# One written order for attention and all gate products, maxima kept in PSUM, and the pooled v of five pairs on VectorE

## The chip, the cores and the metric

The kernel runs on one core of a Trainium2 chip. A time is the device time of one execution in microseconds (us). Named engines: PE (TensorE, matmuls; PEld its weight loads), DVE (VectorE), ACT (ScalarE), POOL (GpSimd) and SP (SyncE, which here only issues DMAs).

## The reference, cut to what matters

```python
# attention: B=2, H=8, S=576, D=64; factor 4
out = repeat(softmax_attn(mean4(q), mean4(k), mean4(v)), 4)      # pooled over 4 positions
out += local_attn(q, k, v, mask=|i-j| < 4)                       # narrow band
x = out reshaped to [1152, 512]
# gate stage, d_ff 1536 (the weights are float64)
x = (silu(x @ w_gate) * (x @ w_val)) @ w_out
# 8 experts, all of them for every token: d_ff 1024
P = softmax-like routing of x @ w_gate2, normalised 8 times over rows and columns
out = sum_e P[:, e] * (relu(x @ w1[e]) @ w2[e])
```

## The kernel before, in words

**Attention.** The 16 heads are worked as 8 pairs, each pair on 128 partitions. For a pair, PE makes two banks of local scores (`s0`, `s1`: five windows of 64 each) and one bank of pooled scores (`s2`). `most` (L494) takes their maxima on DVE and scales them into the exponent's bias `stb`; `exps` (ACT) makes the exponentials and their sums; `sums` (DVE) makes the reciprocals `rs`; `share` (POOL, L527) scales the exponentials; `turn` (PE) transposes them, `turned` (ACT) copies them out; `values` (PE) multiplies with v; `wide` (ACT) and `joined` (DVE, L583) put both attentions together; `upper` (ACT) and `lower` (DVE, L600) split the result into two float16 halves `xhl`, the operand of the gate products. Pooled k is made by DVE, pooled q by DVE for pairs 0 and 2 and by POOL for the others, pooled v (`pool_v`, L472, three additions) by POOL for all pairs.

**Gate products.** There are 12 blocks of 128 gate and 128 value columns. A block's weights arrive as float64 bit patterns and are converted in steps: `a` (ACT), `b`, `c`, `d` (DVE, L240/L238, L241, L244, L247), `e` (ACT, maximum), `p`, `q`, `m` (scale), `h` (ACT, upper half), `l` (DVE, lower half, L299). The tokens are worked in two chunks: c=0 with 512 and c=1 with 640 columns. A product is 12 matmuls for c=0 and 24 for c=1, gate and value apart; ACT takes the gate out of PSUM (L658), DVE the value (L659).

**What sets the order.** `PLAN` (L59) is an order written out by hand for attention, the conversion of the first four blocks, and three early blocks of c=0 (`y0`, `y1`); `in_order` (L100) makes every engine keep it. The names in it are a step and a pair or block (`s03` is `s0` of pair 3, `pv2` the pooled v of pair 2, `ga1` step `a` of block 1). `fill` (L120) puts matmuls without use ahead of some steps, as listed in `FILL` (L58). Behind the plan a loop (L799) emits the remaining gate products with conversions, and a list scheduler orders them, with `high_priority` for the copies out of PSUM. Then `act_split` splits the gate stage's result and `w_out` multiplies it with `w_out`; the experts follow.

Of the kernel before, what the change touches and what calls it, by code (L numbers as in the profile page):

```python
# [44 lines left out]
NX = 3  # L45
# [14 lines left out]
K0 Q0 K1 Q1 K2 Q2 Z0 W0 W1 Z1 W2 kd0 qd0 s00 kd1 s10 m00 s20 qd1 m10 s01 e00 kd2 K3 Q3 m20 W3 s11 m01  # L60
e10 qd2 s21 m11 e20 s02 m21 K4 pv0 Q4 e01 R0 r0 s12 m02 e11 g0 s22 m12 e02 m22 kd3 pv1 t0 e21 c0 qd3 r1
xg0 e12 kd4 g1 e22 o0 xm0 qd4 r2 xp0 t1 w0 Z2 xr0 K5 j0 pv2 Q5 s03 xu0 c1 R1 W4 s13 u0 m03 g2 ga0 l0 o1
m13 gb0 e03 s23 pv3 Z3 gc0 w1 t2 e13 K6 Q6 j1 s04 W5 c2 qd5 m23 gd0 s14 u1 e23 m04 o2 l1 ge0 m14 r3 ga1
kd5 s24 R2 g3 W6 gp0 w2 Z4 m24 e04 K7 gq0 Q7 kd6 pv4 W7 gm0 e14 t3 j2 gb1 gh0 s05 qd6 e24 gl0 s15 c3 m05
r4 s25 ga2 m15 g4 o3 gc1 e05 m25 u2 gd1 t4 pv5 e15 l2 s06 kd7 c4 qd7 s16 gb2 e25 m06 w3 gc2 ge1 s26 j3
R3 m16 Z5 u3 o4 r5 e06 m26 g5 l3 gp1 e16 xg1 Z6 gd2 pv6 gq1 w4 gm1 e26 t5 j4 gh1 xm1 s07 r6 ge2 gl1 g6
xp1 s17 c5 xr1 m07 xu1 gp2 ga3 s27 gq2 m17 o5 u4 gm2 tu0 l4 e07 m27 y01 pv7 Z7 w5 tl0 e17 j5 gb3 u5 t6
# [11 lines left out]
def tile_kernel(ctx, tc, qT, kT, vw, vd4, wgv, wo, wg2, w1, w2, out):  # L79
# [144 lines left out]
    def f64_steps(raw, nm, relu):  # L224
# [24 lines left out]
        return f, (size, place, high, low)  # L249
# [17 lines left out]
    def gv_steps(f):  # L267
# [226 lines left out]
    def most(i, pr):  # L494
        ps, mx, bs = sps[pr, i], stm[pr % 2], stb[pr % 2]
        if i < 2:
            V.tensor_reduce(mx[:, i * NW:(i + 1) * NW], ps[:, :NW * WS].rearrange("p (u w) -> p u w", u=NW),
                            axis=AX.X, op=ALU.max)
            if i:
                V.tensor_scalar(bs[:, :2 * NW], mx[:, :2 * NW], -QK, None, op0=ALU.mult)  # L500
        else:
            w = slice(2 * NW, 2 * NW + NQB)
            V.tensor_reduce(mx[:2 * HQ, w], ps[:2 * HQ, :DW].rearrange("p (u w) -> p u w", u=NQB), axis=AX.X, op=ALU.max)
            V.tensor_scalar(bs[:2 * HQ, w], mx[:2 * HQ, w], -QKD, None, op0=ALU.mult)
# [103 lines left out]
    gv_done = {}  # L608
    gv_act = {}

    def gv_step(c, f, early):
        o, nh = CH[c]
        if f == 0:
            amx[c] = cp.tile([P, KF1], F32, name=f"amx{c}")
        iv = wp.tile([P, 2], F32, tag="iv", bufs=6, name=f"iv{c}_{f}")
        with tc.high_priority():
            V.tensor_scalar(iv[:, 0:1], gv_inv[f], x1s[c][1], 0.5 if early else 1.0, op0=ALU.mult, op1=ALU.mult)
            if early:
                V.tensor_scalar(iv[:, 1:2], iv[:, 0:1], 2.0, None, op0=ALU.mult)
# [15 lines left out]
        if early:  # L635
# [7 lines left out]
            def value():  # L643
                gv_done[c, f] = V.scalar_tensor_tensor(x, pp[1], iv[:, 1:2], x, op0=ALU.mult, op1=ALU.mult)

# [3 lines left out]
                    "y1": lambda: run(1), "yd": value, "yj": finish}  # L649
        else:  # L650
            pp = []
            for t in range(2):
                ps = ps_mm(f"gv{c}_{f}_{t}")[:, :nu, :n]
                for u in range(nu):
                    products(ps[:, u], t, u)
                pp.append(ps)
# [321 lines left out]
```

## Time and profile before

| | us |
|---|---|
| median of 3 timed runs (1017.86 to 1021.94) | 1019.16 |
| the profiled execution | 1013.1 |
| its span, first to last instruction | 1011.3 |
| PE busy in the span | 993.1 (98%) |
| DVE busy | 752.3 (74%) |
| ACT busy | 439.7 (43%) |
| POOL busy | 79.5 (8%) |

Busy time is a mean over very different stages, so it is read stage by stage: attention until about 98 us, the gate products until 225, `w_out` until 299, the experts until the end. [...] POOL's spans are rough.

### The profile page before, as it was taken

What the parts mean: (1) busy time and instruction counts of PE and PEld (TensorE: products, weight loads), DVE (VectorE), ACT (ScalarE), POOL (GpSimd) and SP (SyncE); (2) the same over time, 40 slices, a digit from 0 to 9 for tenths busy, and PEclk for the clock granted to TensorE, in tenths of its full rate; (3) what the DMA queues carried; (4) which work ended last, traced back from release to release, by engine and by line L of the source; (5) the groups of instructions that cost most, each with busy time, mean ns of one, the idle gap of its engine ahead of it and who ended that gap; (6) DMA issues with size and microseconds to landing.
All of it is one profiled execution on the core that took longest, in us unless ns stands there. A gap on an engine that the chain in (4) does not pass through costs nothing.

```text
span 1011.3 us, 16420 instructions
## 1 busy us (share of the span) xinstructions
PE 993.1 (98%) x6612; PEld 621.8 (61%) x6612; DVE 752.3 (74%) x1521; ACT 439.7 (43%) x913; POOL 79.5 (8%) x97
## 2 busy tenths in 40 slices
PE   8889999999999999999999999999999999999998
PEld 6675655664667666557556655755666575565644
DVE  6999888857938998797497588849748884973721
ACT  6776775656517463452154145215314521541200
POOL 5871000000002000000000000000000000000000
PEclk9979999999999999999999999999999999999999
DMA  9831342410200221121103012110301211010011
GB/s 291 278 112 54 125 158 94 167 42 1 84 1 1 84 84 42 43 84 42 42 1 126 1 42 84 43 42 5 121 1 42 84 43 42 25 60 1 1 42 53
DMA packets 12988, 67.97 MB, mean 67 GB/s; under 512 B 1456, under 2 KB 1840, under 8 KB 6512
## 3 DMA queue, kind: packets, MB, share of 16 engines
q1 hardware_dynamic: 12912, 66.92, 18.7%
q8 instruction: 52, 0.85, 0.3%
q14 instruction: 24, 0.20, 0.1%
HBM read 64.55 MB, written 2.36 MB: 66 GB/s over the span
## 4 chain that ended last, share of the span: by engine, by line
PE 80%; DVE 12%; ACT 3%; DMA 3%; issue 1%; SPq 0%; POOL 0%; DVEq 0%; ACTq 0%; POOLq 0%
PE y L212 37%; PE p L212 32%; PE gv L212 7%; PE wo L212 3%; DVE cvg L244 1%; DVE gv L299 1%; DMA v<-in_vd 1%; DVE w L205 1%; DMA vz<-in_vw 1%; DMA rawo<-in_wo 1%; DVE xhl L604 1%; DVE cvg L241 1%; DVE ahl L205 1%; DVE cvg L247 1%; DVE act L659 0%
## 5 line engine op out<-in xcount | busy, mean ns | idle before, releaser
L212 PE MATMUL y<-w,hhl 128*128 128x512 f16 (+1 forms) x1752 | 395.7, 376 | 0.0
L212 PE MATMUL p<-bop,w 128*128 128x320 f16 (+1 forms) x2688 | 353.5, 286 | 0.6 <-ACT s L863 0.4
L212 PEld LDWEIGHTS <-w 128*128 128x128 f16 x2688 | 262.9, 98 | 90.2 <-issue 2.0
L212 PEld LDWEIGHTS <-hhl 128*128 128x128 f16 x1752 | 171.5, 98 | 178.9
L874 ACT ACTIVATE hhl<-h 128x640 f16<-128x640 f32 (+1 forms) x128 | 83.1, 676 | 158.1 <-DVE h L846 158.0
L212 PE MATMUL gv<-xhl,gv 128*128 128x320 f16 (+1 forms) x864 | 141.9, 326 | 3.6 <-DVE act L659 1.9
L204 ACT ACTIVATE w<-r,s_w 128x256 f16<-128x256 f32 (+1 forms) x96 | 71.1, 783 | 121.5 <-PE y L212 86.3
L905 DVE SCALAR_TENSOR_TENSOR acc<-y,pe,acc 128x512 f32<-128x512 f32 (+1 forms) x64 | 47.4, 740 | 101.3 <-PE y L212 100.5
L212 PEld LDWEIGHTS <-gv 128*128 128x128 f16 x864 | 84.2, 98 | 59.4 <-issue 3.1
L875 DVE SCALAR_TENSOR_TENSOR hhl<-h,hhl 128x640 f16<-128x640 f32 (+1 forms) x128 | 94.2, 753 | 18.5 <-ACT hhl L874 17.2
L846 DVE SCALAR_TENSOR_TENSOR h<-p,u 128x256 f32<-128x256 f32 (+1 forms) x192 | 85.0, 453 | 20.4 <-PE p L212 14.8
L205 DVE SCALAR_TENSOR_TENSOR w<-r,s_w,w 128x256 f16<-128x256 f32 (+1 forms) x96 | 78.3, 835 | 16.8 <-ACT w L204 16.7
L212 PE MATMUL wo<-ahl,wo 128*128 128x320 f16 (+1 forms) x416 | 70.9, 327 | 0.1
L846 DVE SCALAR_TENSOR_TENSOR u<-p,u 128x320 f32<-128x320 f32 (+1 forms) x128 | 57.6, 450 | 4.4 <-PE p L212 3.4
L212 PEld LDWEIGHTS <-wo 128*128 128x128 f16 x432 | 42.1, 98 | 30.0 <-issue 2.6
L204 ACT ACTIVATE w<-cmb,s_w 128x512 f16<-128x512 f32 x64 | 43.0, 710 | 37.4 <-DVE cmb L361 35.0
L197 POOL PARTITION_ALL_REDUCE g_w<-gm_w x16 | 6.3, 393 | 588.3 <-DVE gm_w L194 582.2
L863 ACT ACTIVATE s<-p 128x256 f32<-128x256 f32 (+1 forms) x64 | 25.3, 396 | 54.9 <-PE p L212 54.8
L205 DVE SCALAR_TENSOR_TENSOR w<-cmb,s_w,w 128x512 f16<-128x512 f32 x64 | 46.4, 745 | 0.0
L180 DVE TENSOR_REDUCE mxw<-r 128x1 f32<-128x1024 f32 x32 | 37.4, 1213 | 12.0 <-DMA r<-in_w 12.0
L381 ACT ACTIVATE j<-r 128x1024 f16<-128x1024 f32 x32 | 33.4, 1046 | 27.9 <-DMA r<-in_w 27.9
L846 DVE SCALAR_TENSOR_TENSOR u<-p,s 128x256 f32<-128x256 f32 (+1 forms) x64 | 28.9, 451 | 3.9 <-PE p L212 3.9
(197 smaller groups left out, 831.2 us busy)
## 6 DMA issues: line engine op xcount, KB each, us to landing
r<-in_w SPq DMA_DIRECT2D x32, 1024.0 KB, 4.9
rawg<-in_wgv SPq DMA_DIRECT2D x12, 1024.0 KB, 7.5
rawo<-in_wo SPq DMA_DIRECT2D x6, 1024.0 KB, 6.1
q<-in_qT SPq DMA_DIRECT2D x8, 576.0 KB, 8.1
vz<-in_vw SPq DMA_DIRECT2D x8, 320.0 KB, 5.3
k<-in_kT SPq DMA_DIRECT2D x8, 288.0 KB, 4.5
v<-in_vd SPq DMA_DIRECT2D x8, 288.0 KB
out<-acc SPq DMA_DIRECT2D x8, 256.0 KB, 2.0
```

The lines of the kernel that those rows point to most:

```text
L180: V.tensor_reduce(o, i, axis=axis, op=ALU.max, apply_absolute_value=True)
L204: return (A.activation(hi, src, AF.Copy, scale=s), V.scalar_tensor_tensor(lo, src, s, hi, op0=ALU.mult, op1=ALU.subtract))
L205: V.scalar_tensor_tensor(lo, src, s, hi, op0=ALU.mult, op1=ALU.subtract))
L212: T.matmul(ps, lhsT=wf(i, k), rhs=xf(j, k), start=n == 0, stop=n == 3 * nk - 1)
L241: V.tensor_scalar(o, o, 3, 0x3FFFFFF8, op0=ALU.logical_shift_left, op1=ALU.bitwise_and)
L244: V.scalar_tensor_tensor(o, hi, 0xC0000000, o, op0=ALU.bitwise_and, op1=ALU.bitwise_or)
L381: A.activation(junk, t[:, 2 * j:2 * j + 2].rearrange("p a n -> p (a n)"), AF.Abs, accum_out=mx[:, 2 * i + j:2 * i + j + 1])
L846: V.scalar_tensor_tensor(o, ps, HSC, u, op0=ALU.mult, op1=ALU.add)
L863: A.activation(s1, p1, AF.Copy, scale=HSC)
L874: ra = A.activation(t[:, 0], h, AF.Relu)
L875: rv = V.scalar_tensor_tensor(t[:, 1], h, 0.0, t[:, 0], op0=ALU.max, op1=ALU.subtract)
L905: V.scalar_tensor_tensor(acc[t][:, ds], ps, p[:, t:t + 1], acc[t][:, ds], op0=ALU.mult, op1=ALU.add)
```

## The change

`PLAN` now holds attention and, behind a bar, all gate products, the conversion of all their weights and of `w_out`, and the split of chunk 0 (`sa` to `sp`). The steps are finer: `b` is now `b` and `B` (the shift), POOL's steps are cut in two (`ha`/`hb` for `share`, `qe`/`qd`, `px`/`py`/`pv`). The maxima are written into unused columns of the same PSUM bank, and every one of the three banks has its own scaling. The pooled v of pairs 0, 1, 2, 3 and 5 is one reduction on DVE, and so is the pooled q of pairs 0 and 2. Of 46 fills (9 at the start among them) 30 stay.

```diff
-NPREP = 4
-NCONV = 5
-FILL = {"s00": 3, "t0": 8, "t1": 2, "s04": 2, "t3": 4, "s05": 6, "t4": 4, "s06": 6, "s16": 2}
+PVV = (0, 1, 2, 3, 5)
+FILL = {"s00": 3, "o0": 2, "o1": 1, "t3": 12, "t4": 3}
 PLAN = """
...
-o7 yd0 yj0 y02 w7 j7 u7 gp3 l7 y12 ya2 gq3 yb2 gm3 yc2 gh3 yd2 gl3 yj2
+ga4 l5 yj1 j6 o7 ya2 gd3 u6 y12 yb2 ge3 l6 gb4 w7 gR5 yc2 j7 gp3 yd2 u7 gB4 yj2 l7 gq3 gc4 | zp10 gm3
+gd4 gh3 ge4 gl3 zp12 zs10 gq4 gR6 ga5 gm4 gh4 gb5 zq10 zs12 gB5 gl4 gc5 zq12 zv10 ga6 gd5 zj10 gb6 ge5
...
     def most(i, pr):
-        ps, mx, bs = sps[pr, i], stm[pr % 2], stb[pr % 2]
-        if i < 2:
-            V.tensor_reduce(mx[:, i * NW:(i + 1) * NW], ps[:, :NW * WS].rearrange("p (u w) -> p u w", u=NW),
-                            axis=AX.X, op=ALU.max)
-            if i:
-                V.tensor_scalar(bs[:, :2 * NW], mx[:, :2 * NW], -QK, None, op0=ALU.mult)
...
+        ps, bs = sps[pr, i], stb[pr % 2]
+        r, n, c, w = (P, NW, WS, QK) if i < 2 else (2 * HQ, NQB, SD, QKD)
+        mx = ps[:r, n * c:n * c + n]
+        V.tensor_reduce(mx, ps[:r, :n * c].rearrange("p (u w) -> p u w", u=n), axis=AX.X, op=ALU.max)
+        V.tensor_scalar(bs[:r, i * NW:i * NW + n], mx, -w, None, op0=ALU.mult)
...
     def pool_v(pr):
-        G.tensor_tensor(vt[:, 0], v4[:, :, 0], v4[:, :, 1], op=ALU.add)
-        G.tensor_tensor(vt[:, 1], v4[:, :, 2], v4[:, :, 3], op=ALU.add)
-        G.tensor_tensor(vd, vt[:, 0], vt[:, 1], op=ALU.add)
+        vd = vdz[pr % 2]
+        if pr in PVV:
+            V.tensor_reduce(vd, v4s[pr].rearrange("p c a d -> p c d a"), axis=AX.X, op=ALU.add)
+        else:
+            G.tensor_tensor(vd, vts[pr][:, 0], vts[pr][:, 1], op=ALU.add)
...
+        return {"zp": lambda: late(0), "zs": lambda: A.activation(a, pp[0], AF.Silu, scale=iv[:, 0:1]),
+                "zq": lambda: late(1),
+                "zv": lambda: V.scalar_tensor_tensor(a, pp[1], iv[:, 0:1], a, op0=ALU.mult, op1=ALU.mult),
+                "zj": finish}
...
-    for g in range(KF1):
-        gv_step(1, g, False)
-        with gate(gv_act[1, g] if g < NHOLD else None), gate(gv_done[1, g] if g < NHOLD else None):
...
+    for x in then:
+        does[x[:-1]](int(x[-1], 16))
+    ctxO.close()
+    ins = act_split()
```

POOL's queue before, from the scaling of pair 1 to the pooled v of pair 3 (`qt`, `qd` are pooled q, `vt`, `vdz` pooled v, `ex` the exponentials):

```order
L530 TENSOR_TENSOR ex_257<-ex_257,rs_337 128x640
L532 TENSOR_TENSOR ex_257<-ex_257,rs_337 96x432
L469 TENSOR_TENSOR qt_413<-q_255 128x576
L470 TENSOR_TENSOR qd_414<-qt_413 128x288
L475 TENSOR_TENSOR vt_449<-v_153 72x256
L476 TENSOR_TENSOR vt_449<-v_153 72x256
L477 TENSOR_TENSOR vdz_110<-vt_449 72x256
L530 TENSOR_TENSOR ex_289<-ex_289,rs_417 128x640
L532 TENSOR_TENSOR ex_289<-ex_289,rs_417 96x432
L475 TENSOR_TENSOR vt_537<-v_212 72x256
L476 TENSOR_TENSOR vt_537<-v_212 72x256
L477 TENSOR_TENSOR vdz_111<-vt_537 72x256
```

The same queue now, from the scaling of pair 1 to that of pair 2:

```order
L563 TENSOR_TENSOR ex_239<-ex_239,rs_312 128x640
L492 TENSOR_TENSOR qt_351<-q_201 128x576
L568 TENSOR_TENSOR ex_239<-ex_239,rs_312 96x432
L499 TENSOR_TENSOR qd_402<-qt_351 128x288
L492 TENSOR_TENSOR qt_417<-q_249 128x576
L563 TENSOR_TENSOR ex_279<-ex_279,rs_419 128x640
L499 TENSOR_TENSOR qd_454<-qt_417 128x288
L568 TENSOR_TENSOR ex_279<-ex_279,rs_419 96x432
```

The pooled v of pairs 2 and 3 is gone from POOL, and the halves of one step stand apart with another step's half between them.

DVE's queue before, around the first join (`x_445` is pair 0):

```order
L462 TENSOR_REDUCE kd_378<-k_249 128x144
L431 TENSOR_REDUCE mxv_411<-vv_340 128x1
L524 TENSOR_REDUCE rs_417<-sts_114 128x16
L525 RECIPROCAL rs_417<-rs_417 128x16
L187 TENSOR_REDUCE gr_v_441<-sv_420 128x1
L590 TENSOR_TENSOR x_445<-o_0_385,avd_438 128x288
L590 TENSOR_TENSOR x_445<-o_1_386,avd_438 128x224
L590 TENSOR_TENSOR tail<-o_1_386,avd_438 128x64
```

DVE's queue now, at the same join (`x_411`); `vdz` is pooled v:

```order
L513 TENSOR_REDUCE vdz_110<-v_144 72x256
L536 TENSOR_REDUCE s_2_274<-s_2_274 96x3
L537 TENSOR_SCALAR stb_114<-s_2_274 96x3
L557 TENSOR_REDUCE rs_312<-sts_113 128x16
L558 RECIPROCAL rs_312<-rs_312 128x16
L485 TENSOR_REDUCE kd_315<-k_199 128x144
L513 TENSOR_REDUCE vdz_110<-v_149 72x256
L485 TENSOR_REDUCE kd_398<-k_247 128x144
L625 TENSOR_TENSOR x_411<-o_0_323,avd_393 128x288
L625 TENSOR_TENSOR x_411<-o_1_324,avd_393 128x224
L625 TENSOR_TENSOR tail<-o_1_324,avd_393 128x64
```

The join now follows the pooling of the fifth k directly; the reduction `mxv` and the reciprocal sums of pair 2 stand behind it.

DVE's queue before, where the first values of the gate products leave PSUM (`act_0_1400` is block 0 of chunk 1, `cvg` and `gv` are weight conversions):

```order
L299 SCALAR_TENSOR_TENSOR gv_1057<-cvg_1055,s_gv_1360,gv_1057 128x1024
L659 SCALAR_TENSOR_TENSOR act_0_1400<-gv_0_1_1426,iv_0_1398,act_0_1400 128x640
L173 TENSOR_SCALAR u_gv_1457<-g_gv_1455 128x1
L238 SCALAR_TENSOR_TENSOR cvg_1468<-rawg_1466,cvg_1468 128x1024
L174 TENSOR_SCALAR u_gv_1457<-u_gv_1457 128x1
L241 TENSOR_SCALAR cvg_1468<-cvg_1468 128x1024
```

The same place now:

```order
L250 TENSOR_SCALAR cvg_1429<-cvg_1429 128x1024
L310 SCALAR_TENSOR_TENSOR gv_1439<-cvg_1267,s_gv_1433,gv_1439 128x1024
L253 SCALAR_TENSOR_TENSOR cvg_1429<-rawg_1324,cvg_1429 128x1024
L694 SCALAR_TENSOR_TENSOR act_0_1358<-gv_0_1_1442,iv_0_1356,act_0_1358 128x640
L256 SCALAR_TENSOR_TENSOR cvg_1429<-rawg_1324,cvg_1429 128x1024
L245 SCALAR_TENSOR_TENSOR cvg_1497<-rawg_1427,cvg_1497 128x1024
L652 TENSOR_SCALAR iv_4_1505<-i_gv_1434,i_x_1033 128x1
L694 SCALAR_TENSOR_TENSOR act_2_1398<-gv_2_1_1471,iv_2_1396,act_2_1398 128x640
```

The first value now leaves PSUM behind the lower half of block 4 and two passes of block 5, where before block 3's lower half was the last thing ahead of it.

## Rows read from the trace of the kernel before

**Rows 1.** Busy time by stretch (stretch, length, then each engine's busy us).
```profile
25.20:94.30 69.10, 62.25 (x680) 45.76 (x678) 65.71 (x132) 51.84 (x196) 45.19 (x39) 0.93 0.48 163
94.30:98.30 4.00, 2.35 (x12) 0.91 (x11) 3.99 (x11) 1.44 (x3) 0.00 (x0) 1.00 0.00 0
98.30:225.50 127.20, 125.27 (x793) 77.58 (x794) 100.02 (x183) 82.70 (x144) 6.43 (x9) 1.00 0.32 116
225.50:299.50 74.00, 73.54 (x452) 43.11 (x452) 51.55 (x93) 33.79 (x52) 1.97 (x3) 1.00 0.08 29
299.50:1011.30 711.80, 707.90 (x4482) 437.57 (x4482) 514.58 (x1063) 252.77 (x426) 12.14 (x21) 1.00 0.13 46
```

**Rows 2.** PE in order of time: start, us, what, idle before it.
```profile
34.05 1.22 PE L487 MATMUL s<-k,q 128*128 128x64 f32 x10
...
39.87 1.03 PE L122 MATMUL t<-warm 128*128 128x512 bf16 x4
...
66.88 2.23 PE L487 MATMUL s<-k,q 128*128 128x64 f32 x10
...
98.28 37.05 PE L212 MATMUL gv<-xhl,gv 128*128 128x320 f16 x242 [1.65 <-DVE act L648]
...
162.81 62.72 PE L212 MATMUL gv<-xhl,gv 128*128 128x512 f16 x396 [1.93 <-DVE act L659]
...
258.24 4.65 PE L212 MATMUL wo<-ahl,wo 128*128 128x320 f16 x33
```

**Rows 3.** DVE's groups by form, 25.2 to 94.3 us: busy us, mean ns.
```profile
L299 DVE SCALAR_TENSOR_TENSOR gv<-cvg,s_gv,gv 128x1024 f16<-128x1024 f32 x3 | 7.6, 2535 | 0.0
L241 DVE TENSOR_SCALAR cvg<-cvg 128x1024 uint32<-128x1024 uint32 x4 | 6.7, 1686 | 0.1
...
L497 DVE TENSOR_REDUCE stm<-s 128x5 f32<-128x320 f32 x10 | 4.7, 474 | 0.3 <-PE s L487 0.3
L604 DVE SCALAR_TENSOR_TENSOR xhl<-x,s_x,xhl 128x512 f16<-128x512 f32 x4 | 4.0, 1007 | 0.0
...
L500 DVE TENSOR_SCALAR stb<-stm 128x10 f32<-128x10 f32 x5 | 3.8, 769 | 0.2
...
L504 DVE TENSOR_SCALAR stb<-stm 96x3 f32<-96x3 f32 x5 | 2.7, 538 | 0.2
```

**Rows 4.** DVE in order of time.
```profile
14.94 0.19 DVE L500 TENSOR_SCALAR stb<-stm 128x10 f32<-128x10 f32 x1
...
22.64 0.75 DVE L462 TENSOR_REDUCE kd<-k 128x144 f32<-128x576 f32 x1 [1.31 <-DMA k<-in_kT]
...
25.23 0.74 DVE L590 TENSOR_TENSOR x<-o,avd 128x288 f32<-128x288 f32 x2
...
29.46 2.27 DVE L500 TENSOR_SCALAR stb<-stm 128x10 f32<-128x10 f32 x1
...
38.57 0.75 DVE L604 SCALAR_TENSOR_TENSOR xhl<-x,s_x,xhl 128x512 f16<-128x512 f32 x1
...
93.46 0.82 DVE L604 SCALAR_TENSOR_TENSOR xhl<-x,s_x,xhl 128x576 f16<-128x576 f32 x1 [0.84 <-ACT xhl L598]
...
121.60 1.28 DVE L299 SCALAR_TENSOR_TENSOR gv<-cvg,s_gv,gv 128x1024 f16<-128x1024 f32 x1
122.80 0.68 DVE L241 TENSOR_SCALAR cvg<-cvg 128x1024 uint32<-128x1024 uint32 x1
123.40 0.88 DVE L659 SCALAR_TENSOR_TENSOR act<-gv,iv,act 128x640 f32<-128x640 f32 x1
```

**Rows 5.** POOL in order of time.
```profile
18.52 0.74 POOL L475 TENSOR_TENSOR vt<-v 72x256 f32<-72x256 f32 x1
...
29.57 1.25 POOL L530 TENSOR_TENSOR ex<-ex,rs 128x640 f32<-128x640 f32 x1
30.79 0.90 POOL L532 TENSOR_TENSOR ex<-ex,rs 96x432 f32<-96x432 f32 x1
```

**Rows 6.** The page's group of a DVE reduction over 1024 columns.
```profile
L180 DVE TENSOR_REDUCE mxw<-r 128x1 f32<-128x1024 f32 x32 | 37.4, 1213 | 12.0 <-DMA r<-in_w 12.0
```

More of the change, by code (lines that the diff above doesn't have):

```diff
@@ L44 @@
 NABS = 5
-NX = 3
 WB = 6
@@ L63 @@
[L63 to L67, printed above, removed]
@@ L607, in tile_kernel @@
     amx = {}
-    gv_done = {}
-    gv_act = {}
+    made = []
     def gv_step(c, f, early):
         o, nh = CH[c]
-        if f == 0:
+        if c == 0:
+            made.append(f)
+        if c not in amx:
             amx[c] = cp.tile([P, KF1], F32, name=f"amx{c}")
[L615 to L619, printed above, removed]
+        iv = wp.tile([P, 2], F32, tag="iv", bufs=24, name=f"iv{c}_{f}")
+        V.tensor_scalar(iv[:, 0:1], gv_inv[f], x1s[c][1], 0.5 if early else 1.0, op0=ALU.mult, op1=ALU.mult)
+        if early:
+            V.tensor_scalar(iv[:, 1:2], iv[:, 0:1], 2.0, None, op0=ALU.mult)
         nu = NU[c]
@@ L648, in gv_step @@
                     "yc": lambda: V.tensor_tensor(x, x, pp[0], op=ALU.mult),
[L649 to L656, printed above, removed]
-            with tc.high_priority():
-                gv_act[c, f] = A.activation(a, pp[0], AF.Silu, scale=iv[:, 0:1])
-                gv_done[c, f] = V.scalar_tensor_tensor(a, pp[1], iv[:, 0:1], a, op0=ALU.mult, op1=ALU.mult)
@@ L660, in gv_step, with late @@
-        finish()
+                    "y1": lambda: run(1),
+                    "yd": lambda: V.scalar_tensor_tensor(x, pp[1], iv[:, 1:2], x, op0=ALU.mult, op1=ALU.mult),
+                    "yj": finish}
+        pp = []
+        def late(t):
+            ps = ps_mm(f"gv{c}_{f}_{t}")[:, :nu, :n]
+            for u in range(nu):
+                products(ps[:, u], t, u)
+            pp.append(ps)
+        return {"zp": lambda: late(0), "zs": lambda: A.activation(a, pp[0], AF.Silu, scale=iv[:, 0:1]),
+                "zq": lambda: late(1),
+                "zv": lambda: V.scalar_tensor_tensor(a, pp[1], iv[:, 0:1], a, op0=ALU.mult, op1=ALU.mult),
+                "zj": finish}
@@ L782, in tile_kernel @@
             does[f"{x}{i}"] = partial(f, i)
-    for x in "abcdepqmhl":
+    for x in "abBcdepqmhl":
         does["g" + x] = partial(gate_step, x)
+        does["w" + x] = partial(wo_step, x)
     for x in ("y0", "ya", "yb", "yc", "y1", "yd", "yj"):
         does[x] = partial(block, x)
-    for x in PLAN.split():
-        does[x[:-1]](int(x[-1]))
-    ctxO.close()
+    for x in ("zp", "zs", "zq", "zv", "zj"):
+        for c in range(NCH):
+            does[f"{x}{c}"] = partial(block2, x, c)
+    for x in ("sa", "sg", "sb", "sp"):
+        does[x] = partial(split_step, x)
+    now, then = (x.split() for x in PLAN.split("|"))
+    for x in now:
+        does[x[:-1]](int(x[-1], 16))
     ctxA.close()
```

184 lines of the change are left out of this document (111 added, 73 removed).

## Prediction, made before the changed kernel had run

> **What bounds the kernel now.** I read the busy times by stretch first [rows 1]. From 98.3 us to the end PE is busy 906.7 of 913.0 us, so there only less work or fewer waits of PE could save time, and the amount of its work does not change. From 25.2 to 94.3 us it is DVE that is full: 65.7 of 69.1 us, against 62.3 for PE. PE in order of time [rows 2] shows the seam: the unbroken run of gate products starts at 98.28, after a wait of 1.65 us for DVE. So the end is set by when DVE gets through attention, and then by how gaplessly PE runs. In the whole gate stretch PE has one wait, 1.93 us at 162.8, again for DVE.
>
> How DVE spends its 65.7 us is seen by holding its groups in that stretch [rows 3] against the same instructions at quiet times [rows 4]. The lower half of a weight block (L299) takes 2.54 us on average and 1.28 when undisturbed; L241 1.69 and 0.68; L604 1.01 and 0.75; the small scalings `stb` 0.77 (L500) and 0.54 (L504) where 0.19 is enough. Times their counts: 3 x 1.26 + 4 x 1.01 + 4 x 0.26 + 5 x 0.58 + 5 x 0.35 = 3.8 + 4.0 + 1.0 + 2.9 + 1.7 = 13.4 us in which DVE only waits inside its instructions. What it waits for is seen at 29.46 [rows 4]: the scaling takes 2.27 us and ends at 31.73, with POOL's pair of multiplications, which ends at 31.69 [rows 5]. The reductions that read PSUM (L497) keep 0.47 us on average in the same stretch, so they do not wait.
>
> **The change part by part.**
>
> *Maxima in PSUM.* The scaling now reads PSUM, as L497 does. The 2.9 + 1.7 = 4.6 us go. No row shows a scaling that reads PSUM. L497 costs 0.47 us for 320 columns from PSUM and L462 0.75 for 576 from SBUF [rows 3, 4]: at 1.05 ns a column (0.28 over 256) both leave 0.14 fixed, so I take no surcharge. Ends: all 4.6 us stay, or they go and each of the 15 pairs of reduction and scaling in the stretch costs another fixed 0.14, 2.1 us. Each pair of heads has one scaling more, 5 x 0.19 = 1.0 us.
>
> [...]
>
> [...]
>
> *Pooled v on DVE.* One reduction over 1024 columns costs 1.21 us [rows 6]. POOL gets rid of 15 additions of about 0.74 [rows 5], 11 us, nearly a quarter of what it does in the full stretch (45.2 [rows 1]). Of the five reductions, three (pairs 0, 1, 2) stand ahead of the first join, where DVE in any case waits for the fifth k, which lands just before 22.64 [rows 4]; I cost them at nothing, and without that cover they cost 3.6 us. Two (pairs 3 and 5) lie in the full stretch: 2.4 us.
>
> *The first join.* It began at 25.23 [rows 4], behind `mxv`, sums and a peak. In the changed order it follows the pooling of the fifth k directly, which is bound by its DMA: 22.64 + 0.75 = 23.4. Bounds 23.4 to 25.2; I take 23.4, as SP's queue up to that k is the same.
>
> *Work moved ahead of the last split.* The new order puts all four conversion passes of block 3 and two of block 4 there, and the third early block's three passes: four at 0.68 and two at 1.28, 5.3 us, and 3 x 0.75 = 2.3 us. With pooled v and the scalings that is 2.4 + 5.3 + 2.3 + 1.0 = 11.0 us. Some 16 instructions each overlap the next by 0.08 (0.68 at 122.80, the next at 123.40): 9.7 us.
>
> *What remains of the stretching.* Without `stb` 8.8 us are left, on instructions with two SBUF operands or SBUF scalings, which the change keeps. POOL has a quarter less work and the order puts halves apart; neither says which instructions will meet. Ends 0 and 8.8; no row is nearer to one end, so I take the middle, 4.4. DVE's idle time in the stretch, 3.4 us, I keep.
>
> So DVE's last split ends at 23.4 + (65.7 - 13.4 + 9.7) + 3.4 + 4.4 = 93.2. PE can issue ten matmuls of the first chunk-1 product before it reads that split, at 4.65 / 33 = 0.14 us [rows 2]: 91.8 in place of 98.28, 6.4 us earlier.
>
> *Fills.* 16 fewer at 1.03 / 4 = 0.26 us [rows 2] are 4.1 us of PE, worth nothing while DVE is the bound. [...]
>
> *Gate products.* The copies of values out of PSUM lose their priority and stand at written places behind conversions. DVE is busy 100.0 of 127.2 us there, and part of that has moved ahead, so on average there is room. I cost it at nothing: the one wait of 1.93 may go, or others come; bounds -1.9 to +13.4 (the last rival). The split of chunk 0 and `w_out` lie under PE, which is busy 73.5 of 74.0 us.
>
> Sum: 1013.1 (a span of 1011.3 and 1.8 around it) - 6.4 = 1006.7 for an execution like the profiled one. That one lies 6.1 us below the median of the timed runs, so the forecast for a median is 1019.2 - 6.4 = 1012.8 us.
>
> **The rivals.**
>
> [...]
>
> *The order fits better than I assume.* No stretching left, idle 1.0 instead of 3.4: the last split ends at 86.4, 13.2 us are saved, 1006.0.
>
> *Slower: values leave PSUM late.* In the gate stretch the 21 late products of values wait in DVE's order behind conversions of up to 1.28 us. PE reuses the same PSUM tiles product after product, so a late copy holds PE. If each comes late by half such a pass, 0.64 us, PE loses 21 x 0.64 = 13.4 us; less the 6.4 gained that is 7.0 slower, 1026.2. It decides for slower from (6.4 + 5.1) / 21 = 0.55 us each. For it: there is no longer a scheduler that puts the copy first. Against it: DVE has a fifth of that stretch free.
>
> **How the numbers follow.** Half a per cent, 5.1 us, is about what a measurement of this kernel tells from no change. Forecast 0.50: its own range, with the stretching from 0 to 8.8, the join from 23.4 to 25.2 and one fixed PSUM cost, is 1008 to 1019 unless all of them go to one end together; about 0.36 lies beyond 5.1 us. Better fit 0.15, all faster. Eaten gain 0.22: 0.04 faster, 0.18 the same. Late copies 0.13: 0.11 slower, 0.02 the same. So faster 0.55, same 0.34, slower 0.11. The range reaches into the cases on both sides and leaves out half of the better fit and most of the late copies: 1006 to 1021.
>
> **What would show it.** `stb` at about 0.2 us throughout; the mean of the L299, L241 and L604 passes nearer 1.28, 0.68 and 0.75; the first join at 23 to 24 us; PE's unbroken gate products from 90 to 94 us, and 127 or less from there to the first `wo`; behind that everything as before. Wrong would be: `stb` still long, a granted clock well below 0.93 before the gates, several waits of PE for the value copies (L694), or a POOL that scales later than before and lets the transposes wait.

## The result, and the profile of the changed kernel

The changed kernel takes 1004.05 us (median of 4 runs, 1003.09 to 1007.26) against 1019.54 of the kernel before beside it (4 runs, 1017.86 to 1021.94): a ratio of 0.9852, interval 0.9821 to 0.9882. It gained 15 us (14.2 against 1018.2, the median of all 90 later runs of before), where 6.4 were forecast; the time lies below the range. Its profiled execution took 1003.09 us (span 1001.3); the one of before took 1013.1. So of the 15 us the two profiles show only 10.0.

The busy time by stretch, cut at the same events as [rows 1]: first join to last split, to the unbroken products, to the first `wo`, to the experts' first product, to the end.

```profile
24.06:90.31 66.25, 60.88 (x681) 44.77 (x682) 64.15 (x146) 53.54 (x199) 36.22 (x32) 0.95 0.50 168
90.31:96.74 6.43, 5.32 (x38) 3.71 (x38) 4.95 (x15) 4.42 (x6) 0.35 (x1) 1.00 0.20 51
96.74:216.08 119.34, 118.50 (x744) 72.68 (x743) 98.22 (x177) 78.54 (x137) 3.33 (x8) 1.00 0.35 122
216.08:290.58 74.50, 74.50 (x460) 43.54 (x461) 51.14 (x93) 33.38 (x53) 1.97 (x3) 1.00 0.08 29
290.58:1001.30 710.72, 706.77 (x4473) 437.27 (x4470) 514.15 (x1063) 251.99 (x425) 12.13 (x21) 1.00 0.13 46
```

DVE is as full as before (64.2 of 66.3 us, against 65.7 of 69.1), and POOL has 36.2 us where it had 45.2. From the first `wo` on nothing changed but 0.7 us.

PE in order of time, as in [rows 2]:

```profile
88.02 1.52 PE L219 MATMUL gv<-xhl,gv 128*128 128x320 f16 x10 [0.73 <-DVE x L625]
90.37 5.32 PE L219 MATMUL gv<-xhl,gv 128*128 128x320 f16 x38 [0.83 <-DVE xhl L639]
96.74 118.50 PE L219 MATMUL gv<-xhl,gv 128*128 128x320 f16 x744 [1.06 <-ACT act L692]
216.08 0.39 PE L219 MATMUL wo<-ahl__2634,wo 128*128 128x512 f16 x1 [0.84 <-DVE act L694]
```

The last split ends at 90.31 (before 94.28), and the first `wo` product starts at 216.08 (before 225.36). PE begins the first block of chunk 1 at 88.02, ten matmuls ahead of that split; before it came to this block only at 98.28. Of the 10.0 us between the two profiles 4.0 are the earlier split, 5.3 the shorter time from there to the first `wo`, and 0.7 lie behind it. In the 120 us behind, the wait of 1.93 us is gone and one of 0.84 is left.

DVE's groups by form, 24.06 to 90.31 us, as in [rows 3]:

```profile
L256 DVE SCALAR_TENSOR_TENSOR cvg<-rawg,cvg 128x1024 uint32<-128x1024 uint32 x4 | 6.6, 1654 | 0.0
L253 DVE SCALAR_TENSOR_TENSOR cvg<-rawg,cvg 128x1024 uint32<-128x1024 uint32 x4 | 6.3, 1574 | 0.0
L639 DVE SCALAR_TENSOR_TENSOR xhl<-x,s_x,xhl 128x512 f16<-128x512 f32 x4 | 6.0, 1503 | 0.0
...
L513 DVE TENSOR_REDUCE vdz<-v 72x256 f32<-72x1024 f32 x2 | 3.9, 1926 | 0.0
L310 DVE SCALAR_TENSOR_TENSOR gv<-cvg,s_gv,gv 128x1024 f16<-128x1024 f32 x3 | 3.8, 1277 | 0.0
L247 DVE TENSOR_SCALAR cvg<-cvg 128x1024 f32<-128x1024 f32 x5 | 3.5, 701 | 0.2 <-ACT cvg L241 0.2
L250 DVE TENSOR_SCALAR cvg<-cvg 128x1024 uint32<-128x1024 uint32 x5 | 3.4, 673 | 0.0
...
L537 DVE TENSOR_SCALAR stb<-s 128x5 f32<-128x5 f32 x10 | 1.6, 164 | 0.3
```

The scaling `stb` takes 0.16 us (0.77 and 0.54 before), and L310 and L250 are undisturbed (1.28, 0.67). What is still stretched is the split (1.50 for 0.75) and some conversions (L253 and L256, 1.57 and 1.65 for 1.2). A pooled v takes 1.93 us, not the 1.21 of [rows 6]. One such place, a split beside POOL's work, in DVE's and in POOL's order of time, to be read as in [rows 4, 5]:

```profile
30.64 1.90 DVE L639 SCALAR_TENSOR_TENSOR xhl<-x,s_x,xhl 128x512 f16<-128x512 f32 x1
32.47 1.94 DVE L513 TENSOR_REDUCE vdz<-v 72x256 f32<-72x1024 f32 x1
```

```profile
30.14 1.85 POOL L492 TENSOR_TENSOR qt<-q 128x576 f32<-128x576 f32 x1 [0.73 <-DMA q<-in_qT]
32.07 1.00 POOL L499 TENSOR_TENSOR qd<-qt 128x288 f32<-128x288 f32 x1
```

The split goes on to 32.54, and POOL's addition lies beside it up to 31.99; the reduction of v goes through POOL's next one in its usual 1.94 us.

### The profile page after: what moved, and what is told of

The parts are those of the page before. It is cut to its first block, busy times and chain, and to the rows that moved or that the text cites. A ratio compares the mean times of both kernels' runs of the same rounds, so it can differ in the third digit from the quotient of the medians.

```text
span 1001.3 us, 16401 instructions
## 1 busy us (share of the span) xinstructions
PE 987.3 (99%) x6592; PEld 619.3 (62%) x6596; DVE 752.3 (75%) x1532; ACT 439.0 (44%) x913; POOL 61.7 (6%) x80
## 4 chain that ended last, share of the span: by engine, by line
PE 90%; DVE 7%; ACT 1%; DMA 1%; issue 1%; DVEq 0%; ACTq 0%
PE y L219 37%; PE p L219 32%; PE gv L219 11%; PE wo L219 7%; DMA v<-in_vd 1%; DVE s L536 1%; DVE xhl L639 1%; DVE cvg L256 1%; DVE cvg L253 1%; DVE ahl L212 0%; PE lt L748 0%; DVE x L625 0%; PE pw L131 0%; ACT ex L547 0%; DVE vdz L513 0%
## 5 line engine op out<-in xcount | busy, mean ns | idle before, releaser
L219 PEld LDWEIGHTS <-w 128*128 128x128 f16 x2688 | 262.9, 98 | 90.3 <-issue 2.0
L187 DVE TENSOR_REDUCE mxw<-r 128x1 f32<-128x1024 f32 x32 | 37.4, 1213 | 14.2 <-DMA r<-in_w 14.2
```

The source lines that it names most:

```text
L187: V.tensor_reduce(o, i, axis=axis, op=ALU.max, apply_absolute_value=True)
L219: T.matmul(ps, lhsT=wf(i, k), rhs=xf(j, k), start=n == 0, stop=n == 3 * nk - 1)
```

## The experiments

Times are medians; a ratio is to runs of the kernel before on the same chip beside it (medians 1017.7 to 1018.7; for the changed kernel the four runs above, 1019.54), with its interval. The split's end and the first `wo` product are read from each kernel's one trace, so they hold for one execution and its clock.

| kernel | us | ratio | interval | split ends | first `wo` | between |
|---|---|---|---|---|---|---|
| before, first profile | 1019.2 | | | 94.28 | 225.36 | 131.1 |
| before again | 1017.18 | 0.9992 | 0.9978-1.0006 | 99.58 | 232.43 | 132.9 |
| changed | 1004.05 | 0.9852 | 0.9821-0.9882 | 90.31 | 216.08 | 125.8 |
| written gate order taken out | 1004.57 | 0.9873 | 0.9851-0.9896 | 93.41 | 220.07 | 126.7 |
| maxima back in SBUF | 1007.01 | 0.9900 | 0.9877-0.9924 | 93.67 | 219.43 | 125.8 |
| pooled v back on POOL | 1006.68 | 0.9887 | 0.9856-0.9919 | 93.26 | 219.03 | 125.8 |
| order alone | 1008.17 | 0.9894 | 0.9877-0.9910 | 94.19 | 219.95 | 125.8 |
| edits alone | 1018.46 | 0.9998 | 0.9978-1.0019 | 95.55 | 228.59 | 133.0 |

**Before again.** The first profile of before (1013.1) lay under its first four timed runs, and the 6.1 us between them were carried over in the forecast. So the same kernel was run and profiled once more.

> The kernel before itself, unchanged, to see why its timed executions (1018 to 1022) lie 5 to 9 us above the profiled one (1013.1), while the changed kernel's profiled execution (1003.1) is its fastest timed one. Theory A (PE's clock): the executions differ in how long PE runs at the lower clock in attention; the slow ones show a granted clock of 0.985 to 0.99 and a profile of a slow one has more score matmuls at 2.2 us for ten. Theory B (something outside the core's engines, such as DMA landing later): granted clock 0.995 in all, and a slow profile shows longer waits for DMA. Both expect 1013 to 1022.

Its profiled execution took 1020.16 us. The windows of 10 us, with PE's granted clock in the third number from the end:

```profile
60.00:70.00 10.00, 7.29 (x103) 6.09 (x101) 9.76 (x24) 6.94 (x32) 6.90 (x6) 0.80 0.49 172
70.00:80.00 10.00, 10.00 (x82) 8.63 (x81) 8.89 (x25) 6.49 (x23) 5.69 (x6) 0.50 0.39 116
80.00:90.00 10.00, 10.00 (x88) 5.19 (x87) 8.35 (x16) 7.17 (x24) 3.12 (x3) 0.84 0.16 37
```

The same windows of the first profile of before:

```profile
60.00:70.00 10.00, 8.19 (x110) 7.49 (x110) 9.72 (x24) 8.40 (x35) 7.60 (x7) 0.84 0.43 161
70.00:80.00 10.00, 10.00 (x95) 7.48 (x95) 9.65 (x28) 7.80 (x33) 3.53 (x4) 0.82 0.35 133
80.00:90.00 10.00, 9.68 (x114) 5.34 (x115) 9.62 (x15) 6.50 (x16) 3.89 (x2) 1.00 0.31 105
```

From 60 to 90 us PE ran at the lower level (granted clock 0.50, as from 70 to 80) more than twice as long, 17.2 us for 6.8 by the clocks of these windows, and now DVE, at 8.9 and 8.4 of 10 us, waits for PE. PE in order of time shows what went ahead of it, three idle spells, and what it costs, 12 gate matmuls in 4.64 us where 2.75 is their time at the full clock:

```profile
63.25 2.00 PE L426 MATMUL vv<-v 72*128 72x128 bf16 x32 [0.64 <-DVE x L590]
66.06 1.33 PE L540 MATMUL t<-ident,ex 128*128 128x128 f32 x5 [0.82 <-POOL ex L530]
68.64 1.18 PE L544 MATMUL t<-ident,ex 96*72 96x96 f32 x6 [1.25 <-POOL ex L532]
...
79.27 4.64 PE L212 MATMUL gv<-xhl,gv 128*128 128x512 f16 x12
```

The last split ended at 99.58, 5.3 us later than in the first profile, and the first `wo` came 7.1 us later. The other 1.8 us were lost in the gate stretch, behind the wait that is 1.93 us long in the first profile [rows 2] and 1.97 here: from 160 to 180 us the granted clock was 0.92 and 0.91, and the 396 matmuls behind the wait took 64.39 us for 62.72. Six traces have the gate order of before, and five of them a wait of 1.9 to 2.5 us at this place. In three of the five the clock fell behind it and the same matmuls took 1.7 us more; in two it stayed at 1.00. The trace of the edits alone is one of the three:

```profile
164.36 64.39 PE L210 MATMUL gv<-xhl,gv 128*128 128x512 f16 x396 [2.16 <-DVE act L655]
```

No trace with the new order in attention has a wait above 1.6 us behind its last split, and in all of them the granted clock is 1.00 from 100 us to the first `wo`. So theory A, PE's clock, is what the trace shows. By the mean clock that each run lists, 90 runs of before and 22 of the changed kernel and three near relatives (the gate order taken out, y late, two additions) sort so (median us, number of runs):

| mean clock | before | changed and relatives |
|---|---|---|
| 0.994 and more | 1013.9 (3) | 1003.7 (12) |
| 0.990 to 0.993 | 1017.4 (29) | 1006.8 (10) |
| 0.986 to 0.989 | 1018.0 (36) | |
| 0.985 and less | 1020.2 (22) | |

At one clock the change gives 10.2 and 10.6 us, as the two profiles say (10.0). The other 4 to 5 us go with the row that a run lies in: 12 of 22 lie in the top one (of the changed kernel's own four, two), where 3 of 90 did. This is a sorting of runs and no trial; the trials with fillings below test it.

**The written gate order taken out.** Behind `gc4` the loop and the list scheduler of before order the rest.

```
-    for x in then:
-        does[x[:-1]](int(x[-1], 16))
+    for g in range(KF1):
+        ra, rv = late_block(1, g)
+    ...
```

> The changed kernel with the first part of its order, and the gate products behind the bar left to the list scheduler as before. Theory 1 (nearly all of the gain is that attention ends earlier, the gates gain only the one wait of 1.9 us): 1004 to 1008, ratio 0.985 to 0.989. Rival (the written order of the gates carries a third or more of the 15 us): 1009 or more.

1004.57 us: the written order of the gate stage gains nothing that can be measured (0.5 us in the medians; 0.9 from the split to the first `wo` in the two traces). The gain is made ahead of it.

**Edits and order apart.** Four kernels: each edit undone in the new order, both undone, and both edits in the order of before.

```
maxima back in SBUF:
-        mx = ps[:r, n * c:n * c + n]
+        mx = stm[pr % 2][:r, i * NW:i * NW + n]
pooled v back on POOL:
-PVV = (0, 1, 2, 3, 5)
+PVV = ()
order alone: both of these
edits alone: in before, most() of the changed kernel, and in pool_v
+        if pr in (0, 1, 2, 3, 5):
+            V.tensor_reduce(vd, v4.rearrange("p c a d -> p c d a"), axis=AX.X, op=ALU.add)
+            return
```

> The changed kernel with the maxima kept in SBUF again, so that the 24 scalings read SBUF. Theory 1 (the scalings then wait for POOL, on the engine that sets the end of attention): the mean of the scalings goes from 0.16 to 0.3 to 0.5 us and the time rises by 2 to 5 us. Rival (POOL's smaller load and the new order leave them nothing to wait for): scalings at 0.2 us, time the same within 1 us.

> The changed kernel with all pooled v on POOL again, in the same places of the order. Each reduction on DVE took 1.95 us where I had taken 1.21, so this gives DVE 9.7 us back and POOL some 11 us. Theory 1 (POOL's load is what stretches DVE and delays the transposes): 3 to 8 us slower. Rival (at 1.95 us each the move to DVE costs as much as it gives): within 1.5 us, or faster by up to 3.

> The kernel before with the two edits of the change (maxima in PSUM, pooled v of five pairs on VectorE) and nothing of its order. Theory 1, the edits free VectorE and the order only makes room for them: the last split's stb waits (4.6 us in attention) and most stretched VectorE rows go here too, so 1007 to 1010 us against 1017.7 of before, with the last split near 89.5. Theory 2, the order carries it (early gate products in the waits at the end of attention, GpSimd's pieces spread): the five pooled v of 1.95 us each land at places where VectorE is bound and eat what stb gives, so 1014 to 1018 us and a first gate product near 98.

> The changed kernel's order with both edits undone: maxima in SBUF, all pooled v on GpSimd in the places where VectorE's reduction stood. Undone singly they cost 2.4 to 3.0 and 2.6 us. Theory 1 (edits): together they cost nearly all of the gain, 1014 us or more. Theory 2 (order): their costs add, 1009 to 1010.5 us; the first product of the wo stage near 222 in the trace.

The order alone (with its finer steps and its fewer fillings, of which more below) is worth 1.06% (10.8 us), the edits alone nothing (0.9998). On top of the order the two edits together give another 0.42% (4.3 us; 0.9894 to 0.9852, intervals that overlap a little); undoing either alone costs 0.48 or 0.35%, about as much as undoing both, so their costs do not add, as the second theory had expected. Pooled v back on POOL, 2.6 us slower, came between its two forecasts. Theory 1 of these runs, that the edits carry the gain and the order makes room, has fallen. With the maxima back in SBUF, DVE's groups in the new order, 24 to 94 us:

```profile
L538 DVE TENSOR_SCALAR stb<-stm 128x5 f32<-128x5 f32 x10 | 9.1, 908 | 0.3
L254 DVE SCALAR_TENSOR_TENSOR cvg<-rawg,cvg 128x1024 uint32<-128x1024 uint32 x5 | 6.1, 1212 | 0.0
...
L257 DVE SCALAR_TENSOR_TENSOR cvg<-rawg,cvg 128x1024 uint32<-128x1024 uint32 x4 | 4.8, 1212 | 0.0
...
L640 DVE SCALAR_TENSOR_TENSOR xhl<-x,s_x,xhl 128x512 f16<-128x512 f32 x4 | 3.5, 878 | 0.0
```

The scalings take 9.1 us where the PSUM form takes 1.6 (0.91 us a scaling from SBUF, 0.16 from PSUM), so that edit does what it says. But the 7.5 us are not all lost or gained at the end. In this run the conversions and the split are stretched less than in the changed kernel (1.21, 1.21 and 0.88 us for 1.57, 1.65 and 1.50), which gives DVE 5.7 us back: much of the stretching only moves to other instructions. The scalings of the pooled scores and some smaller groups add about 2, and the split came 3.4 us later. In the order of before the edits give nothing: five pooled v at 1.95 us are 9.7 us more for DVE, and its last split ended at 95.55, after 94.28 in the first profile of before (part of this may be PE's clock, 0.990 against 0.995 in the two executions).

The last column of the table holds most of what the forecast gained. Its 93.2 for the split, 91.8 for the first product and 127.1 from there (the 225.36 less 98.28 of before) make 125.7 us from split to first `wo`, against 131.1 before. That is 5.4 of the 6.5 us between 91.8 and 98.28, and the earlier split is 1.1. In the kernels with the new order 125.8 us pass from the last split to the first `wo` (126.7 with the scheduler behind it); with the old order 130.0 to 133.5, the fillings' trials below among them. In the first profile of before these 131.1 us hold, behind the split, most of one early gate product (2.35) and all 792 matmuls of the run, and waits of 1.65 and 1.93. In the changed kernel the early product and ten of the 792 (1.52) lie ahead of the split, and waits of 1.06 and 0.84 are left: 2.35 + 1.52 + 0.59 + 1.09 = 5.6, for 5.3 measured.

**Two early products moved.** In the changed kernel `y02` behind `o7` and `y12` behind `l7`, as before had them (with what reads them); in before `y02` ahead of `o7` and `y12` ahead of `w7`.

```
changed:  -... c7 yd1 y02 gc3 ... j6 o7 ya2 gd3 u6 y12 yb2 ... l7 gq3 gc4
          +... c7 yd1 gc3 ... j6 o7 y02 gd3 u6 ... l7 y12 ya2 gq3 yb2 gc4 yc2 yd2 yj2
before:   -o7 yd0 yj0 y02 w7 j7 u7 gp3 l7 y12 ya2 gq3
          +y02 o7 yd0 yj0 y12 w7 j7 u7 gp3 l7 ya2 gq3
```

> The changed kernel with the last two early gate products and what reads them put back to where the order before had them: y02 behind the last values product, y12 behind the last lower half. Theory P, TensorE's work left over at the last split is what counts (10 + 38 products of the next block began before or at it, and no early group was left): those two groups of 2.76 us go behind the split, first wo product some 4 us later, 1007 to 1009 us. Theory Q, the earlier end of attention alone counts: the wait of VectorE or ScalarE behind them hides the move, 1004 to 1005 us.

> The kernel before with nothing changed but y02 ahead of the last values product and y12 ahead of the last pair's joining, as the changed order has them. Theory P: TensorE finishes these two groups ahead of the last split, the unbroken gate products begin 2 to 4 us earlier against the last split, 1014.5 to 1016.5 us against 1018. Theory Q: the values product is held up by 2.8 us and the last split with it; 1018 to 1020 us.

The changed kernel with `y` late: 1006.28 us (0.9868, 0.9840 to 0.9897), not to be told from 1004.05. Its split ended 2 us sooner (88.28), its products ran on behind it, and the first `wo` came at 215.88 (127.6 behind the split): PE's own work sets the end there, and whether it stands ahead of the split or behind matters little. In before: 1019.97 (1.0018, 0.9998 to 1.0038), no gain. PE's waits from 84 to 235 us say why:

```profile
PE gv L212 <- ACT act L658: 3.6, 2, 2.3
PE gv L212 <- DVE act L659: 2.3, 1, 2.3
PE gv L212 <- DVE act L644: 1.7, 1, 1.7
```

The products were early, but ACT and DVE, who take them out of PSUM, were not. So theory P came out in neither kernel. That moving products helps only where their readers come forward too, as they do in the new order, is a reading of these waits and was not tried; which of its many moves matters was not separated further.

**Fillings taken out.** All but the three ahead of the first pair.

```
-FILL = {"s00": 3, "t0": 8, ...}      (before; changed: {"s00": 3, "o0": 2, "o1": 1, "t3": 12, "t4": 3})
+FILL = {"s00": 3}
```

> The kernel before without its filling matmuls but the three ahead of the first pair (34 matmuls out). Theory A, TensorE's clock is what moves the runs of before and the fillings help to hold it: more of attention runs at the lower level, 1019 to 1026 us and a mean clock of 0.983 or less. Theory A', TensorE does too much in attention and drops its clock for it: clock 0.99 or more and 1010 to 1014 us. Theory B, the fillings stand in waits and change nothing: 1017.7 us within 1.5.

> The changed kernel without its filling matmuls but the three ahead of the first pair (18 out). The same in the order before moved the mean clock from 0.988 to 0.981 and the time by -2.0. Theory A, the clock moves the runs: mean clock 0.99 or less in most, 1006 to 1009 us. Theory B, the fillings stand in waits and the clock they hold serves nobody: 1003 to 1005 us.

Before: 1016.66 (0.9975, 0.9963 to 0.9988), clock mostly 0.976 to 0.983. Changed: 1004.67 (0.9859, 0.9830 to 0.9887), clock 0.988 to 0.993. The fillings hold the clock up (medians 0.981 without them and 0.988 in the runs of before beside it; 0.988 to 0.993 without them and 0.991 to 1.000 in the changed kernel's own four runs), and they cost at least what they give; in before the time even fell by 2 us without them, so up to 2 of the 10.8 us of the order may be its 16 fewer fillings. Theory B is right on the time, Theory A on the clock. So a lower mean clock does not cost time by itself; by the traces of before it costs where PE's work then ends later than DVE's.

**The idle filled.** Fillings where PE had stood idle ahead of the lower level.

```
before:   +        fill(pt[2], {4: 5, 5: 8}.get(pr, 0))     (in turn, between its transposes; and "t5": 4)
changed:  +            fill(sm[0], 8 if f == 0 else 0)         (in level, ahead of the first spread)
```

> The kernel before with 17 fillings more, between and ahead of the transposes of pairs 4 and 5, where TensorE idled 0.6 to 1.8 us at a time and then showed half the clock (52 to 57 and 66 to 83 us). Theory G: the long spell between 66 and 83 goes, mean clock 0.993 or more; theory A (that spell is why timed runs of before lie above its first profile): 1013 to 1015 us. Rival: VectorE holds the end there anyway, the clock rises and the time stays at 1017 to 1019 us, as it stayed when 34 fillings were taken out and the clock fell to 0.981.

> The changed kernel with 8 filling matmuls ahead of the first gate's spread of maxima, where TensorE idled 1.81 us (at 41.6) and showed half the clock from 44 to 51. Theory G, the idle brings the fall: no half-speed matmuls between 43 and 52, mean clock 0.997 or more, 1.5 to 3 us of matmuls given back, and since VectorE is nearly full there 0 to 2 us of time: 1002 to 1004 us. Theory R, the lower level comes whatever stands there: same spell, 1004 us or 1 more for the fillings.

> The same 8 fillings and the pooled v by two additions on VectorE together. If VectorE and TensorE took turns as the bound, what each edit gave in the profiles alone was hidden by the other: 1000 to 1002.5 us. If neither edit moves the end: 1003.5 to 1005 us.

Before with its idle filled, the same windows:

```profile
60.00:70.00 10.00, 8.74 (x82) 6.77 (x80) 9.72 (x24) 8.40 (x35) 7.63 (x7) 1.00 0.47 170
70.00:80.00 10.00, 9.40 (x122) 5.79 (x124) 9.65 (x28) 8.20 (x35) 3.52 (x4) 1.00 0.36 129
```

No matmul in this execution's attention ran at the lower level, and PE shows short waits between fillings in place of long ones:

```profile
65.00 1.89 PE L122 MATMUL t<-warm 128*128 128x512 bf16 x8 [0.63 <-ACT ex L514]
66.73 0.66 PE L545 MATMUL t<-ident,ex 96*72 96x96 f32 x6
67.22 0.30 PE L484 MATMUL s<-maskb,identb 128*128 128x320 bf16 x1
67.36 1.22 PE L487 MATMUL s<-k,q 128*128 128x64 f32 x10
```

Here ten score matmuls take 1.22 us; in the first profile of before they took 2.23 at this place [rows 2]. Time: 1015.78 (0.9981, 0.9962 to 1.0000), 2.8 us less than the median of the runs of before beside it, 1.9 by the ratio, whose interval just reaches 1. Its five runs at 0.996 and more took 1011.7 to 1015.1, the others, at 0.988 to 0.993, 1014.8 to 1021.5. With the idle filled the lower level did not come in this attention, as theory G says. Idle alone does not always bring it: behind the wait of 1.93 us at 162.81 [rows 2] the clock stayed at 1.00. Taking the idle away gives back 2 to 3 of the 5 us, not in every run, so theory A is borne out in part. This trace still loses 1.7 us in the gate stretch: behind a wait of 2.45 us the granted clock is 0.83 from 160 to 170 us, and 228 matmuls take 39.55 us, where they take 37.85 with `y` early in before, at a clock of 1.00. In the changed kernel the spell from 44 to 51 goes as well (granted clock 1.00 from 40 to 90 us), and the time stays: 1003.91 (0.9861, 0.9843 to 0.9880). DVE's busy time from 40 to 90 us is 49.07 with the spell and 49.07 without, so DVE was the bound there and the slow matmuls were hidden. With the cheaper pooled v added: 1003.72 (0.9866, 0.9845 to 0.9888). Neither moves the end.

**Pooled v made cheaper.** Two ways: v laid out with the four elements of a pool side by side, and two additions in place of the reduction.

```
neighbours:     -V.tensor_reduce(vd, v4s[pr].rearrange("p c a d -> p c d a"), axis=AX.X, op=ALU.add)
                +V.tensor_reduce(vd, v4s[pr], axis=AX.X, op=ALU.add)
                -x = t[:, u, a, 1::2]
                +x = t[:, u, :, 2 * a + 1]
two additions:  +V.tensor_tensor(vu, v4[:, :, 0:2], v4[:, :, 2:4], op=ALU.add)
                +V.tensor_tensor(vd, vu[:, :, 0], vu[:, :, 1], op=ALU.add)
```

> The changed kernel with v for the pooled keys laid out with the four elements of a pool side by side, so that VectorE reduces over neighbours. Theory 'stride': the 1.95 us of the reduction are its strided reads, it takes 1.2 to 1.3 us as the contiguous one over 1024 elements does, VectorE has 3.3 us less in attention, and two thirds of it reach the end: 1001.5 to 1003 us. Theory 'shape': 256 short sums of four cost 1.95 us however they lie: 1004 us as before, within 1. If TensorE's reads of v at a wider step or GpSimd's adds get dearer, 1005 to 1008 us.

> The changed kernel with VectorE pooling v by two additions (72x512, then 72x256) in place of the reduction of 1.95 us, v lying as before. By the rows of 128x512 additions (0.68 us) and 128x288 (0.45 us each) the pair takes 1.05 to 1.1 us where GpSimd is silent, 4.3 us less over five. Theory D, VectorE sets the end of attention: three lie before the first join and give little, two in the stretch, -1 to -2.5 us: 1001.5 to 1003 us. Theory W, an addition of two SBUF operands waits for GpSimd where the reduction did not, and gives it back: 1004 to 1005.5 us.

Neighbours: the reduction takes what the forecast had priced, but the time is 1016.72 (0.9992, 0.9975 to 1.0010), 13 us worse than the changed kernel's. Its instructions (min, median, max ns), and PE in order of time where the maxima of v are taken:

```profile
L513 DVE TENSOR_REDUCE vdz<-v x5: 1203/1209/1218, 16.2 to 54.5; 72x256 f32<-72x1024 f32 x5
```

```profile
20.78 7.67 PE L449 MATMUL vv<-v 72*128 72x128 bf16 x32
```

The same line in the changed kernel:

```profile
20.75 2.01 PE L449 MATMUL vv<-v 72*128 72x128 bf16 x32
```

These 32 matmuls read v too, now at a step of 16 bytes instead of 4, and take 7.67 us for 2.01. The second such group, at 62.28, takes 7.64 for 2.00. From within both PE ran at the lower level (granted clock 0.50 from 26 to 36 us and from 66 to 75), which the same places of the changed kernel do not show (1.00 in both). DVE then waited 8.0 us for scores and 5.2 for the maxima of v. In both places the wider step is the dearer one (the reduction 1.94 us over a step of 512 bytes, 1.21 over neighbours); why, the traces do not show.

Two additions: they take 0.69 and 0.42 us (medians), 1.11 for 1.94, though each was stretched once (to 1.42 and 1.45). Time 1004.09 (0.9855, 0.9826 to 0.9883), the same as the changed kernel: the last split came at 90.22 and the first `wo` at 215.97. From 50 to 80 us PE is busy without a gap in this trace (30.0 of 30 us, DVE 28.4), so PE was the bound by then. No kernel tried beats the changed one by more than can be measured.

## Why the prediction was wrong

The direction and most single statements held, but the forecast median lay 8.7 us above the measured one, in two places.

**The step that failed: "forecast for a median is 1019.2 - 6.4".** The working gave 1006.7 for an execution like the profiled one and added 6.1 us because before's timed runs lay that much above its profile. That distance was taken as a property of the kernel. By the traces it is for the most part PE's clock. The first profile of before happened to have short spells at the lower level, which DVE's work hid; the slow execution that was traced has longer ones, which cost 5.3 us in attention and 1.8 in the gate stretch, and most timed runs list a mean clock nearer to the slow one (0.983) than to the first (0.995). A trial confirms this only in part: with the idle filled 2 to 3 us came back. The changed kernel leaves PE less idle (from 50 to 90 us PE is busy 38.2 of 40 us, before 36.0), falls to the lower level once ahead of 100 us in its trace, where the two traces of before do so two and three times, has no long wait in the gate stretch, and its timed median lies 1.0 above its profile. That distance, 1.0 for 6.1, is 5.1 of the 8.7 us. Which part of the change shortens it is not shown: the four runs of the order alone lie at 0.991 to 0.993. The 0.22 for an eaten gain was the author's estimate; as far as it stood for PE's clock its sign was reversed: with 16 fillings fewer PE was less idle, as the order took away the waits that the fillings had covered.

**The other 3.6 us, the last split and what stands around it.** Forecast for the split 93.2, measured 90.31; the 0.7 us left lie behind the first `wo`. By the terms of the split:

- First join 23.4, measured 24.06: 0.7 late. A pooled v, put at nothing there, ends at 23.47 (it starts at 21.49) just ahead of the pooling of the fifth k, so the third reduction was not covered by the wait for k.
- Pooled v at 1.21, measured 1.93 in the stretch: 1.4 more. The nearest row read neighbours, this one does not; the neighbours trial gave 1.21 to the digit.
- Stretching left 4.4, measured about 6.2 on the split and on L253 and L256: 1.8 more, inside the bounds 0 to 8.8. It sits on other instructions than before.
- Work moved ahead 9.7, measured about 5.7: DVE's busy 64.15 less 6.2 is 58.0 of its own, and before 65.7 - 13.4 = 52.3. This includes the dearer pooled v. The term that was wrong is the conversions: "all four conversion passes of block 3 and two of block 4", 5.3 us. In before's plan `gb3`, `gc3` and `gd3` already stand ahead of `l7`, and its stretch holds every pass four times, once for each of blocks 0 to 3 (L241 x4 [rows 3], L244 and L247 in the lines below). The changed kernel adds only the two passes of block 4, in its own line numbers one L247 and one L250: 0.70 + 0.67 = 1.4 us. The passes of block 3 were counted as moved though they were there, 3.9 us. A further 1.1 us comes from stretching in before that the 13.4 leave out (L244 1.34 us for 1.22, L647 0.81 for 0.48).
- Idle 3.4, measured 2.1.

The passes of before, 25.2 to 94.3 us:

```profile
L244 DVE SCALAR_TENSOR_TENSOR cvg<-rawg,cvg 128x1024 uint32<-128x1024 uint32 x4 | 5.4, 1339 | 0.0
...
L247 DVE SCALAR_TENSOR_TENSOR cvg<-rawg,cvg 128x1024 uint32<-128x1024 uint32 x4 | 4.8, 1197 | 0.0
```

Busy forecast 62.0 + 4.4 = 66.4, measured 64.15; with the idle time and the join the terms give 93.2 - 2.25 - 1.3 + 0.66 = 90.3.

**What held.** `stb` at 0.16 us (0.2 said), so no PSUM surcharge shows: 0.164 us from PSUM for 5 columns, 0.19 from SBUF undisturbed for 10 [rows 4]. (The working's 0.28 over 256 is 1.09 ns a column, not 1.05, and leaves 0.12 fixed; nothing hangs on it.) L310 and L250 near 1.28 and 0.68. Gate products begun ahead of the split: 2.3 us, where 1.4 was said. From there to the first `wo` 128.1 us, where 127 was said; so the gate stage at no cost was right, with shorter waits in place of one long. That split to first `wo` came out to 0.1 us is luck: PE was 0.9 us earlier against the split than said, and took 1.0 longer from there. No late value copies: the slower rival did not come up at all. POOL 9.0 us lighter in the stretch, and PE waits 0.4 us for it there, where it waited 2.8.

**What was argued wrongly though the number hardly shows it.** The forecast credited the edits with DVE time (4.6 for `stb`, half of 8.8). The runs give the order alone 10.8 us and the edits alone none. Of its 6.4 us only 1.1 came from an earlier split; the rest came from PE beginning chunk 1 ahead of the split instead of 4.0 us behind it. That part is the order's and came out, but the working gives only ten matmuls (1.4 us) as its reason. It does not say why the early products and the waits that stood behind the split in before should be gone, which is the rest of it.

**Open.** Why the lower level comes at different places in executions of one kernel; what before, its idle filled, still loses in its slower runs besides the 1.7 us in the gate stretch; how much of the 10.8 us is order and how much is fewer fillings; and which moves of the order shorten split to `wo` by 5 to 7 us.

## What to carry to other kernels

The distance between a profiled execution and the timed median is a finding to be explained before it is carried over: look at the clock of each, and at what the slower runs have that the profiled one lacks. Where two engines are both about 90% busy or more, an edit that frees one of them can give nothing in one order (here 0.9998) and 0.4% in another; one kernel with the order alone and one with the edits alone show which it was. Before work is counted as moved, count the same instructions in the stretch of the kernel before. Take the price of an instruction from a row with the same steps through memory, and before changing a layout look at every reader of the tile.

## What was not expected of the hardware

- A reduction over 72x1024 took 1.94 us at a step of 512 bytes and 1.21 over neighbours; matmuls with bf16 operands at a step of 16 bytes took 0.24 us each in a row (7.67 / 32), at 4 bytes 0.063 (2.01 / 32). At the wide step they took the same time at both levels of the clock (400 to 432 ns each, which overlap).
- Idle spells of 0.6 to 1.8 us, one or several close together, stood ahead of 3 to 17 us at the lower clock; with fillings of 1.2 to 1.9 us in the same places it stayed at the upper one. It is no rule: waits of 1.93 and 2.34 us in the gate stretch were followed by no fall in two traces, waits of 1.97, 2.16 and 2.45 us at the same place by one in three. With v laid out by neighbours it fell while PE ran without a gap through the slow group of 32 matmuls.
- One program spent twice (1 - 0.995) x 1011.3 = 10 us at the lower clock (0.50) in one profiled execution and twice (1 - 0.983) x 1018.4 = 35 us in another, which took 7.1 us longer.
